# First block's list of work ordered anew, its first two groups of attention cut into three parts

## The chip, the cores and the metric

One core of one Trainium2 chip runs the whole program. The metric is the device time of one execution in microseconds (us); lower is better. In the traces PE is TensorE's matrix multiplication, PEld its weight loads, DVE is VectorE, ACT ScalarE, POOL GpSimd, and SP the engine whose queue issues most DMAs. A "product" below is one matrix multiplication instruction with a moving operand of 512 columns, unless it says idle product (128 columns of fp32).

## The reference, cut to what matters

```python
def _attn_ref(q, k, v):                      # 8 batches, 8 heads, 576 tokens, 64 dims
    scores = scale * np.matmul(q, k.transpose(0, 1, 3, 2))
    # heads 0-3: the last 32 positions; heads 4-7: every 32nd position, both causal
    scores = np.where(masks[None], scores, -1000000000.0)
    scores = scores - np.max(scores, axis=-1, keepdims=True)
    attn = np.exp(scores)
    attn = attn / (np.sum(attn, axis=-1, keepdims=True) + 1e-09)
    return np.matmul(attn, v)

def _moe_ref(x, w_in, w_out):                # 4608 tokens, 512 -> 2048 -> 512
    h = x @ w_in
    g = h * (1.0 / (1.0 + np.exp(-h)))
    return g @ w_out
```

The attention's output, 4608 tokens of 512 features, is the x of the second part. Only the banded or strided keys of a query are computed.

## The kernel before, in words

The 4608 tokens are nine blocks of 512. Every fp32 factor of the large products is split into a high and a low part, so that one true product is three products of rounded parts. Block 0 differs from all later ones: while it runs, the weights are still being loaded, split and kept. Its work is not ordered by a planner inside the program but by a list written out by hand or found by a search, the string `PLAN` (line 143). `Steps.follow` goes through that list word by word and issues each step's instructions; each engine then runs its own instructions in the order of the list, waiting only on what they need. A suffix names the engine of a step that can run on several (`.A` ACT, `.D` DVE, `.P` POOL). After block 0 a planner orders the rest; that order does not depend on the list.

The words of the list. For a group c of attention: `k` loads its queries and keys (SP; the queries of groups 0 to 2 go through ACT's queue), `v` its values, `S` the scores (PE, line 485), `M` adds the mask, finds the row's peak and moves the scores to SBUF (DVE, line 513, two instructions for each of the group's three or four columns of tiles), `E` the exponentials (ACT, line 531, as many), `R` sums and reciprocal (DVE, lines 546 and 547), `N` scales (line 550), `T` transposes (PE, line 556), `P` copies the transposed tile out of PSUM (line 560), `O` multiplies by the values (PE, lines 595 and 600), `Q` scales the local groups' result (DVE, line 639), `X` turns it back (PE, line 662), `B` stores it into x (lines 671 and 655). Groups 0 to 2 are local, 3 to 5 strided; groups 6 to 13 belong to blocks 1 and 2 and have `V`, `F`, `G` in place of `T` and `P`. `C` spreads shared values on POOL (lines 411 to 414). `H` and `L` split x (lines 688 and 692).

For a piece i of the weights: `p` loads it, `a` rounds it on ACT (lines 312 and 317), `j` joins (DVE, line 323), `b` casts the high part (line 368), `d` subtracts for the low part (line 372). For a column fc of the hidden layer: `h` and `i` are its two halves of six products each (line 700), `t`, `g`, `w`, `l` the activation and its split, `o` twelve products into the output (line 759). `z` and `u` store split weights to DRAM for later blocks (SP). `~n` is n idle products with the identity (line 872).

Limits that the list must respect: a load into a key buffer waits for the scores that read it last (group 11 shares its buffer with group 9, so `k11` follows `S9`); a piece's stage waits for the `d` of the piece before it; SP issues in the order of the list. `make_identity` and the masks are made on POOL at the start, in the order: the identity, the plain local mask, its copy for tiles that start a head (used by group 0's first column), another copy, the strided mask.

The last part of `Steps.follow` and of `idle`:

```python
            name, _, engine = word.partition(".")
            step = self[name]
            step.engine = next(e for e in step.costs if e.startswith(engine))
            step.act()
```

Of the kernel before, what the change touches and what calls it, by code (L numbers as in the profile page):

```python
# [25 lines left out]
STRIDE = 32  # L26
# [122 lines left out]
M8 l0.D b2.A S7 i3 a7 k10 a4 p11 j6 d2.D w1.A b6.D j7 j4 t2 b7.A o0 p8 g2 b4.A a9 a11 d7.D d4.D  # L149
l1.D j9 M7 w2.A h4 p13 o1 b9.A l2.D p10 j11 d9.D a8 b11.D t3 i4 p15 E8 g3 d6.D t4 d11.D V6 a10  # L150
S10 w3.D j8 p17 a13 g4 h5 p12 F6.A j10 o2 j13 R8 b10.D b8.A h6 d8.D i5 b13.A l3.D G6.A v6 w4.D
d10.D a15 t5 a17 l4.D i6 p14 u1 M10 a12 j15 p16 u0 j17 d13.D b15.D t6 g6 g5 o3 E7 h7 O6 b17.D
d17.D k9 N8.D a16 w6.A p19 B6 o4 d15.D j12 j16 b12.D h8 l6.D p23 d12.D a14 w5.A b16.D j14 E10 i7
l5.D h9 d16.D V8 t7 p21 R10 a19 k12 b14.D v8 j19 a23 o5 i9 R7 j23 g7 a21 F8.A j21 b23.A i8 G8.A
# [62 lines left out]
def sparse_attention_ffn(ctx: ExitStack, tc: tile.TileContext, kqt, vt, w_in, w_out, out):  # L217
# [214 lines left out]
    class Attention:  # L432


        def __init__(self, b, at):
            self.b, self.at, self.gi = b, at, order_of(b)[at]
            self.by_blocks = b * NG + at >= TURNED
            self.g = g = GROUPS[self.gi]
# [28 lines left out]
        def scores(self, banks=None):  # L467
            g, kbd = self.g, self.kbd
            self.pss = banks or [self.bank("pss") for _ in range(2)]
# [12 lines left out]
            for t, c, rows in self.tiles:  # L482
                for h in range(2):
                    at = slice(h * D, (h + 1) * D)
                    nc.tensor.matmul(  # L485
                        self.pss[h][rows, c * self.seen : (c + 1) * self.seen],
                        kbd[at, 1, g.q0[t] : g.q0[t] + g.rows],
                        kbd[at, 0, g.k0[t] : g.k0[t] + self.seen], start=True, stop=True,
                    )

        def peak(self, part=None):
            g = self.g
            s_ps = self.halves(self.pss)
            if part:
                self.peaks_of(s_ps, (part,))
# [168 lines left out]
        def done(self, engine="ACT"):  # L664
            flat = place_of(self.b).rearrange("p n s -> p (n s)")
            x0 = self.g.first * STRIDE
            dst = flat[:, x0 : x0 + self.cols].rearrange(
                "p (r c q) -> p c r q", c=self.g.n, q=STRIDE
            )
            src = self.psx[:, : self.cols].rearrange("p (c r q) -> p c r q", c=self.g.n, q=STRIDE)  # L670
# [120 lines left out]
    def attention_steps(c, due, last=None):  # L791
# [7 lines left out]
        k = add(f"k{c}", {"SP": P * cols * 4 / RATE}, t0 - 6, [], lambda: load_qk(a),  # L799
                writes=[k_place])  # L800
        s = add(f"S{c}", {"PE": 0.75 if local else 0.68}, t0, [k], a.scores, takes=["ps"] * 2)
        steps.reads(s, k_place)
        m = add(f"M{c}", {"DVE": 0.07 + (0.31 if a.wide else 0.27) * n}, t0 + 1,
                [s, wide_masks] if a.wide else [s], a.peak, takes=["sm", "sum"],
                gives=[s])
        u = m
        if a.spread:
            u = add(f"U{c}", {"POOL": 0.35 + 0.21 * n}, t0 + 1.5, [m], a.lessen)
        cost = 0.1 + 0.11 * n if a.spread else (0.73 if a.wide else 0.667) * n
        e = add(f"E{c}", {"ACT": cost}, t0 + 2, [u], a.weigh)  # L810
# [1636 lines left out]
```

## Time and profile before

| what | value |
|---|---|
| median of 3 runs | 807.0 us (807.0 to 807.51) |
| the profiled execution's own time | 805.44 us |
| its span, first to last instruction | 803.7 us |
| mean granted TensorE clock | 1.000 |
| busy: PE, DVE, ACT, POOL | 99%, 75%, 73%, 14% |
| DMA, mean over the span | 238 GB/s |

Busy shares are means over stages that differ. PE's share counts idle products and matmuls whose ends are modelled. Block 0, the part that the list orders, lies in about the first 130 us. Times in the rows are counted from the first instruction. A timeline row gives the start, the length, the engine, the line, the operation, output and input, the shape and the count, and in brackets the idle time before it and what ended that.

### The profile page before, as it was taken

The numbers are of one execution on the slowest core, as the hardware profiler recorded it, in microseconds if no ns is written. First come the engines' busy times: TensorE is split into PE (matmuls) and PEld (weight loads), VectorE is DVE, ScalarE is ACT, GpSimd is POOL, SyncE is SP. The second block draws the span as 40 slices with busy tenths as digits, with TensorE's granted clock in tenths as the row PEclk, the third lists the DMA queues.
The fourth block names the chain that finished last, engine by engine and source line by source line (L and its number), as shares of the span: only waits on it lengthen the run. The fifth ranks groups of instructions, "written<-read, shape, count | busy, mean of one in ns | idle before, by whom it ended". The sixth has DMA issues, their size and how long they took to land.

```text
span 803.7 us, 18907 instructions
## 1 busy us (share of the span) xinstructions
PE 794.1 (99%) x6661; PEld 658.9 (82%) x6661; DVE 599.2 (75%) x1653; ACT 587.3 (73%) x1574; POOL 112.5 (14%) x160
## 2 busy tenths in 40 slices
PE   8999999999999999999999999999999999999998
PEld 5788778888889898888887888888888888888887
DVE  6999985667878889856779999653799945557653
ACT  7999987557689978898885997788846435545551
POOL 6400004667000000015203000000230000000000
PEclk9999999999999999999999999999999999999999
DMA  8888995566977767899987877986677696666776
GB/s 268 289 271 275 286 287 184 207 235 217 298 244 255 235 225 259 245 323 298 289 263 215 282 249 195 257 266 195 179 192 221 193 272 194 193 196 194 190 218 157
DMA packets 150910, 191.13 MB, mean 238 GB/s; under 512 B 38241, under 2 KB 91105, under 8 KB 150817
## 3 DMA queue, kind: packets, MB, share of 16 engines
q1 hardware_dynamic: 149296, 189.21, 77.1%
q8 instruction: 53, 0.87, 0.4%
q10 hardware_dynamic: 1520, 0.72, 0.3%
q14 instruction: 41, 0.33, 0.1%
HBM read 151.09 MB, written 38.80 MB: 236 GB/s over the span
## 4 chain that ended last, share of the span: by engine, by line
PE 93%; DMA 3%; DVE 1%; ACT 1%; SPq 0%; issue 0%; ACTq 0%
PE ps L1579 34%; PE po L2177 20%; PE po L759 16%; PE ps L700 11%; PE ps L2177 6%; PE ps L615 2%; DMA k<-kqt 1%; PE po L2325 1%; DMA stage<-w_in 1%; PE ps L485 1%; PE ps L476 1%; PE po L615 1%; DMA stage<-w_out 1%; PE po L476 0%; DVE stage L2157 0%; PE po L485 0%
## 5 line engine op out<-in xcount | busy, mean ns | idle before, releaser
L1579 PE MATMUL ps<-xop,w 128*128 128x512 f32 (+1 forms) x720 | 143.7, 348 | 0.0
L1579 PE MATMUL ps<-w,w 128*128 128x512 f32 x576 | 138.6, 390 | 0.0
L1579 PEld LDWEIGHTS ps<-xop,w 128*128 128x128 f32 x720 | 118.1, 189 | 18.5
L1579 PEld LDWEIGHTS ps<-w,w 128*128 128x128 f32 x576 | 107.9, 188 | 22.5
L531 ACT ACTIVATE sm<-sm,sums 128x54 f32<-128x54 f32 (+2 forms) x320 | 109.5, 346 | 5.4 <-DVE sums L513 5.0
L2177 PE MATMUL po<-stage,w 128*128 128x512 f32 x456 | 106.4, 390 | 0.0
L2177 PEld LDWEIGHTS po<-stage,w 128*128 128x128 f32 x456 | 85.4, 188 | 17.8
L700 PE MATMUL ps<-xop,w 128*128 128x512 f32 x384 | 94.0, 392 | 0.0
L700 PEld LDWEIGHTS ps<-xop,w 128*128 128x128 f32 x384 | 71.4, 188 | 15.6 <-DVE th L732 0.4
L531 ACT ACTIVATION_READ_ACCUMULATOR sm<-sm,sums 128x1 f32 x320 | 61.0, 191 | 0.0
L759 PE MATMUL po<-w,ghi 128*128 128x512 f32 x168 | 52.2, 392 | 0.0
L2153 ACT CAST stage<-w 128x512 fp32r<-128x512 f32 x54 | 33.5, 621 | 21.2 <-DVE stage L2157 8.8
L2157 DVE TENSOR_TENSOR stage<-w,stage 128x512 fp32r<-128x512 f32 x54 | 40.0, 745 | 11.2 <-ACT stage L2153 10.6
L2015 DVE TENSOR_TENSOR w<-ps,w 128x512 f32<-128x512 f32 x43 | 29.4, 687 | 24.7 <-PE ps L1579 24.2
L744 DVE TENSOR_TENSOR glo<-th,ghi 128x512 fp32r<-128x512 f32 x48 | 38.4, 803 | 8.6 <-ACT ghi L740 7.0
L582 ACT COPY pt<-sm 32x192 f32<-32x192 f32 (+1 forms) x114 | 41.4, 363 | 4.2 <-DVE sm L574 2.0
L2053 ACT ACTIVATE w<-w 128x512 f32<-128x512 f32 x44 | 27.0, 629 | 17.5 <-DVE w L2015 17.3
L2177 PE MATMUL ps<-stage,w 128*128 128x512 f32 x168 | 39.3, 391 | 0.0
L2177 PEld LDWEIGHTS ps<-stage,w 128*128 128x128 f32 x168 | 31.4, 188 | 6.6
L503 POOL MEMSET sm<- 128x80 f32 (+1 forms) x18 | 2.9, 161 | 239.6 <-ACT pt L582 91.7
L732 DVE SCALAR_TENSOR_TENSOR th<-th,ps 128x512 f32<-128x512 f32 x32 | 21.8, 684 | 19.5 <-ACT th L710 19.4
L2011 ACT COPY w<-ps 128x512 f32<-128x512 f32 x47 | 27.4, 586 | 11.9 <-PE ps L1579 10.7
(327 smaller groups left out, 1629.1 us busy)
## 6 DMA issues: line engine op xcount, KB each, us to landing
w<-sums SPq DMA_DIRECT2D x208, 256.0 KB, 3.3
w<-osums SPq DMA_DIRECT2D x160, 256.0 KB, 3.0
sums<-xop SPq DMA_DIRECT2D x16, 512.0 KB, 3.7
osums<-stage SPq DMA_DIRECT2D x16, 512.0 KB, 5.7
v<-vt SPq DMA_DIRECT2D x21, 384.0 KB, 5.2
stage<-w_out SPq DMA_DIRECT2D x14, 512.0 KB, 4.7
k<-kqt SPq DMA_DIRECT2D x14, 477.0 KB, 5.9
stage<-w_in SPq DMA_DIRECT2D x12, 512.0 KB, 4.9
```

The costliest lines, as they stand in the source:

```text
L531: nc.scalar.activation(out=self.s_sb[:, c, h], in_=self.s_sb[:, c, h], func=AF.Exp, bias=self.peaks[:, c, h : h + 1], scale=-1.0, accum_ou ...
L582: copy[by](out=self.pt[to, odd], in_=of)
L700: nc.tensor.matmul(ph, weight(0, wi, fc)[:, cc // 2, cc % 2 * P : (cc % 2 + 1) * P], x[xi][cc], start=(cc, n) == (0, 0), stop=(cc, n) == ( ...
L744: either[engine].tensor_sub(out=g[1][:, cols], in0=th[:, cols], in1=g[0][:, cols].bitcast(F32))
L759: nc.tensor.matmul(po[tt], g[gi][:, cols], weight(1, wi, fc), start=first and n == 0, stop=last and n == 2,)
L1579: nc.tensor.matmul(bank[:, : right.shape[-1]], left(wi, kt), right[:, kt, xi], start=first and (kt, n) == (0, 0), stop=(kt, n) == (1, 2), ...
L2011: copy_ps(out=unit(place), in_=of())
L2015: nc.vector.tensor_add(out=to, in0=of(), in1=to)
L2053: nc.scalar.activation(out=unit(out), in_=source(), func=AF.Silu)
L2153: copy_ps(out=gated_ops(to.slot)[0], in_=unit(place))
L2157: nc.vector.tensor_sub(out=lo, in0=unit(place), in1=hi.bitcast(F32))
L2177: nc.tensor.matmul(bank(name, key, m), left[:, wi, m * P : (m + 1) * P], right[xi], start=first and (j, i) == (0, 0), stop=(j, i) == (FH - ...
```

## The change

Group 0 gets a class of its own, `Opening`. Its keys and queries lie in DRAM as three parts, one for each of its three columns of four tiles: each part holds 160 columns of keys and 128 of queries, 288 columns of 128 partitions, 144 KB. Before, the keys were one DMA of 208 KB and the queries one of 192 KB. The steps of groups 0 and 1 are cut by column: `S0`, `S51`, `S52` are the scores of group 0's columns, `M0`, `M51`, `M52` and `E0`, `E51`, `E52` theirs in turn; `S1`, `S61`, `S62` and so on are group 1's, which is still loaded as a whole. `k0` and `k52` are issued by SP, `k51` by ACT. The number of scores, of mask and peak instructions and of exponentials stays. Idle products: 25 in place of 24, four in front in place of seven. The rest of the list has the same steps in another order; 27 steps change between ACT and DVE. Code for a spread form that no group used is taken out.

```diff
+class Opening(Group):
+    def __init__(self):
+        super().__init__(True, 0, 12)
+        nk, nq = KW + 3 * STRIDE, 4 * STRIDE
+        self.part = nk + nq
+        self.at = [(t // 4, t % 4) for t in range(self.count)]
+        self.k0 = [self.part * c + STRIDE * r for c, r in self.at]
+        self.q0 = [self.part * c + nk + STRIDE * r for c, r in self.at]
+        self.starts = [(0,), *[()] * (self.n - 1)]
...
+PARTED = (0, 1)
...
 PLAN = """
-k0 k1 k2 v0 ~7 S0 v1 M0 k4 E0 k3 v2 C0 ~1 S1 k5 M1 E1 ~3 S2 M2 p1 E2 v5 T0 P0.D R1 ~7 S4 O0 R0
-M4 E4 Q0 k6 C1 v3 v4 T1 P1.D R2 S3 M3 E3 X0 B0.D a1 T2 P2.D O1 p0 C2 Q1 R4 N4.P S5 M5 k7 O2 X1
-Q2 B1.A R3 N3.D ~2 j1 T4 P4.A E5 H00.D p3 p4 k8 X2 B2.A T3 P3.D a0 L00.P H01.A O4 p5 p2 O3 S6
-b1.D B4 R5 N5.D d1.D j0 b0.A L01.P T5 P5.D d0.D p6 B3 H02.D L02.D ~4 O5 B5 H03.D L03.D a3 M6 j3
-b3.D E6 h0 d3.D Y0 h1 i0 t0 R6 a5 g0 i1 h2 w0.A S8 p7 i2 p9 t1 N6.D j5 b5.D d5.D a2 g1 a6 j2 h3
...
-w7.D d14.D d23.D p22 t9 l7.D p18 z3 z0 a22 t8 o6 N7.D g9 j22 p25 u2 g8 b19.A N10.D S9 V7 O8 a18
-b21.A b22.A F7.A j18 k11 d22.D B8 p20 d19.D p24 z2 z1 M9 d21.D v7 a25 w8.D j25 E9 a20 o7 b25.A
-b18.D h10 d18.D l8.D G7.A S11 V10 a24 i10 d25.D j20 R9 p27 u3 M11 t10 j24 F10.A b24.A h11 g10
...
-g12 p28 z6 R12 N12.D G9.A B10 i13 l11.D w12.A V12 O9 k13 a29 l12.D t13 h14 R11 v11 u7 u6 u5 z7
...
-M13 o12 B11 H10.D H11.D L10.D p30 h15 E13 w14.A H12.A a30 p31 L11.D l13.D R13 l14.D L12.D H13.A
+k0 k51 k52 ~4 S0 M0 S51 M51 S52 ~1 k1 M52 S1 k2 M1 E0 v0 C0 ~2 k4 S61 S62 v1 E51 E52 R0 M61 M62
+T0 E1 E61 S2 E62 ~4 C1 k3 M2 S4 T1 R1 P0.D O0 v2 k5 M4 E2 S3 Q0 P1.D X0 E4 M3 B0.D O1 Q1 S5 T2
+v4 p0 v3 P2.D E3 C2 R2 R4 M5 R3 p1 N4.P E5 ~4 a0 X1 p3 O2 ~3 T4 Q2 N3.D X2 P4.D B1.D v5 R5 H00.D
+~7 T3 j0 O4 B2.A N5.D T5 a1 H01.D P3.A k6 b0.D a3 j1 B4 O3 P5.D d0.D j3 B3 O5 b1.D B5 L00.P
+H02.A p2 H03.A a2 S6 b3.D d1.D L01.P d3.D L02.D p5 p4 a5 h0 L03.D M6 h1 j2 b2.D j5 i0 d2.D Y0 k8
+h2 a4 p7 t0 j4 b5.D E6 g0 b4.A p6 d5.D p9 a6 i1 u0 w0.D p8 l0.D i2 p11 d4.D t1 u1 p10 k7 t2 j6
...
+g7 p20 h9 d22.D p21 B6 g8 a23 V10 G8.A w8.D d19.D S9 w7.A j23 M9 l7.D h10 b23.D i9 a20 N7.D
+F10.A d23.D a21 j21 t9 l8.D G10.A d18.D j20 i10 v8 p24 t10 o7 g9 k11 z6 g10 b21.A a24 p25 O8 E9
+k12 j24 z7 S11 d21.D b24.D o8 w10.D B8 d24.D h11 p26 V7 h12 b20.A R9 a25 l10.D F7.A M11 E11 S12
...
+d28.D o11 v11 g13 G11.A O11 z5 a29 j29 b29.D E13 d29.D w13.D R13 i14 z1 N13.D t14 B11 H10.A
+H11.A g14 h15 l13.D L10.D p30 H12.A a30 H13.A o12 p31 L11.D z2 L12.D j30 i15 w14.D t15 b30.D
+l14.D o13 d30.D L13.D a31 j31 b31.A z0 g15 w15.A d31.D l15.D o14 F12.A V13 G12.A F13.A G13.A
...
+    def load_part(i):
+        some = slice(i * OPENING.part, (i + 1) * OPENING.part)
+        way = nc.scalar.dma_start if i == 1 else load
+        way(out=flat_of(kbds[0])[:, some], in_=flat_of(kqt[0, 0])[:, some])
...
+        if first and a.at in PARTED:
+            es, ss, ms = [], [], []
+            for i in range(n):
+                name = 10 * c + 50 + i if i else c
+                if not i or a.g is OPENING:
+                    size = a.g.part if a.g is OPENING else cols
+                    k = add(f"k{name}", {"SP": P * size * 4 / RATE}, t0 - 6, [],
+                            (lambda i=i: load_part(i)) if a.g is OPENING else lambda: load_qk(a),
+                            writes=[] if i else [k_place])
+                s = add(f"S{name}", {"PE": 0.25}, t0, [k, *ss], lambda i=i: a.scores(only=i),
+                        takes=[] if i else ["ps"] * 2)
+                steps.reads(s, k_place)
+                m = add(f"M{name}", {"DVE": 0.29}, t0 + 1, [s, *ms], lambda i=i: a.peak(only=i),
+                        takes=[] if i else ["sm", "sum"])
+                e = add(f"E{name}", {"ACT": 0.667}, t0 + 2, [m, *es], lambda i=i: a.weigh([i]))
+                ss, ms, es = [*ss[:1], s], [*ms[:1], m], [*es, e]
```

## Rows read from the trace of the kernel before

**Rows 1.** The page's first section: busy time and share of the span.

```profile
PE 794.1 (99%) x6661; PEld 658.9 (82%) x6661; DVE 599.2 (75%) x1653; ACT 587.3 (73%) x1574; POOL 112.5 (14%) x160
```

**Rows 2.** Waits of PE, first 135 us: total, times, longest.

```profile
PE ps L485 <- DMA k<-kqt: 1.0, 1, 1.0
```

**Rows 3.** Chain that ended last, 10 to 150 us: start, length, what.

```profile
41.63 1.36 PE ps L700 x6
42.99 2.72 PE po L759 x12
...
76.90 5.80 DMA k<-kqt
```

**Rows 4.** Busy time of each engine in one stretch of five microseconds.

```profile
20.00:25.00 5.00, 4.53 (x127) 3.37 (x126) 4.64 (x10) 4.80 (x18) 2.19 (x2) 1.00 0.96 305
```

**Rows 5.** Timeline of PE, first 135 us.

```profile
1.35 3.15 PE L872 MATMUL ps<-ident 128*128 128x512 f32 x4 [1.35 <-POOL ident masks.py:199]
4.46 0.72 PE L485 MATMUL ps<-k 64*32 64x64 f32 x48
...
8.53 1.67 PE L872 MATMUL ps<-ident 128*128 128x512 f32 x4
...
22.23 0.72 PE L485 MATMUL ps<-k 64*32 64x64 f32 x48
...
24.81 0.91 PE L600 MATMUL po<-pt,v 64*64 64x54 f32 x24 [0.29 <-ACT xb L655]
25.65 7.11 PE L700 MATMUL ps<-xop,w 128*128 128x512 f32 x30
...
82.83 0.58 PE L485 MATMUL ps<-k 64*64 64x64 f32 x24 [0.98 <-DMA k<-kqt]
...
119.61 0.95 PE L759 MATMUL po<-stage,ghi 128*128 128x512 f32 x2
...
120.63 0.63 PE L759 MATMUL po<-stage,ghi 128*128 128x512 f32 x2
```

**Rows 6.** Timeline of ACT: the first exponential.

```profile
5.60 0.35 ACT L531 ACTIVATE sm<-sm,sums 128x64 f32<-128x64 f32 x1 [2.16 <-DVE sums L513]
```

**Rows 7.** Timeline of DVE, 5 to 25 us.

```profile
5.33 0.22 DVE L513 CUSTOM_DVE_ANT_0 sm<-ps,mask 128x64 f32<-128x64 f32 x1 [5.33 <-PE ps L485]
...
8.24 0.22 DVE L513 CUSTOM_DVE_ANT_0 sm<-ps,mask__94 128x64 f32<-128x64 f32 x1 [0.43 <-PE ps L485]
...
10.13 0.52 DVE L546 TENSOR_SCALAR sums<-sums 128x6 f32<-128x6 f32 x1
...
13.39 0.62 DVE L546 TENSOR_SCALAR sums<-sums 128x6 f32<-128x6 f32 x1
...
15.27 0.55 DVE L671 COPY xb<-po 128x384 f32<-128x384 f32 x1
...
16.73 0.16 DVE L546 TENSOR_SCALAR sums<-sums 128x8 f32<-128x8 f32 x1
...
20.05 0.42 DVE L688 CAST xop<-xb 128x512 fp32r<-128x512 f32 x1
20.38 0.68 DVE L560 COPY pt<-po 128x512 f32<-128x512 f32 x1
20.98 1.12 DVE L368 CAST w<-stage 128x512 fp32r<-128x512 f32 x1
...
22.92 0.69 DVE L372 TENSOR_TENSOR w<-stage,w 128x512 fp32r<-128x512 f32 x1
...
24.17 0.54 DVE L560 COPY pt<-po 128x384 f32<-128x384 f32 x1
```

**Rows 8.** Timeline of POOL: a mask's last instruction, then two longer steps.

```profile
4.12 0.23 POOL L253 TENSOR_SCALAR_AFFINE_SELECT mask<-mask 32x64 f32<-32x64 f32 x1
...
17.31 1.04 POOL L550 TENSOR_TENSOR sm<-sm,sums 128x512 f32<-128x512 f32 x1 [3.33 <-DVE sums L513]
20.55 1.27 POOL L692 TENSOR_TENSOR xop<-xb,xop 128x512 fp32r<-128x512 f32 x1 [2.19 <-DVE xop L688]
```

More of the change, by code (lines that the diff above doesn't have):

```diff
@@ L131 @@
 NG = len(GROUPS)
+class Opening(Group):
[7 more added lines that the diff above has]
+        self.starts = [(0,), *[()] * (self.n - 1)]
+OPENING = Opening()
+PARTED = (0, 1)
 def order_of(b):
@@ L150 @@
[L150 to L154, printed above, removed]
-w7.D d14.D d23.D p22 t9 l7.D p18 z3 z0 a22 t8 o6 N7.D g9 j22 p25 u2 g8 b19.A N10.D S9 V7 O8 a18
@@ new lines @@
+H02.A p2 H03.A a2 S6 b3.D d1.D L01.P d3.D L02.D p5 p4 a5 h0 L03.D M6 h1 j2 b2.D j5 i0 d2.D Y0 k8
+h2 a4 p7 t0 j4 b5.D E6 g0 b4.A p6 d5.D p9 a6 i1 u0 w0.D p8 l0.D i2 p11 d4.D t1 u1 p10 k7 t2 j6
+a9 g1 b6.D d6.D u2 j9 w1.A l1.D R6 a7 a8 h3 p12 o0 S8 j7 i3 o1 b9.A g2 a11 b7.D M8 d7.D t3 j11
+a10 g3 z4 b11.A w3.A w2.A d9.D j8 h4 j10 b10.A b8.A p13 S7 a12 h5 l3.D l2.D N6.D E8 i4 d11.D
+d10.D d8.D p15 i5 M7 j12 V6 o2 b12.D a13 p16 h6 j13 t5 t4 a15 d12.D b13.A g5 u4 g4 j15 a16 u3
+w4.D b15.D k10 d13.D u5 l4.D E7 R8 F6.A p14 o3 i6 d15.D h7 p17 w5.D S10 j16 o4 R7 b16.D p18 p19
@@ new lines @@
+t6 a14 d16.D G6.A p22 N8.D i7 u7 v6 l5.D a17 a18 g6 k9 M10 E10 w6.D j17 j14 j18 b14.A a22 h8
+b17.D a19 l6.D d17.D p23 o5 t7 V8 i8 t8 O6 d14.D j22 F8.A R10 o6 j19 b22.A b18.A N10.D b19.A u6
+g7 p20 h9 d22.D p21 B6 g8 a23 V10 G8.A w8.D d19.D S9 w7.A j23 M9 l7.D h10 b23.D i9 a20 N7.D
+F10.A d23.D a21 j21 t9 l8.D G10.A d18.D j20 i10 v8 p24 t10 o7 g9 k11 z6 g10 b21.A a24 p25 O8 E9
+k12 j24 z7 S11 d21.D b24.D o8 w10.D B8 d24.D h11 p26 V7 h12 b20.A R9 a25 l10.D F7.A M11 E11 S12
+j25 w9.D b25.D i12 N9.D d25.D v10 G7.A l9.D t12 a26 d20.D v7 p27 M12 j26 i11 o9 t11 g11 g12
@@ L382, in vbd_of, with flat_of @@
         return at % (VBUFS if b else VFIRST)
+    def load_part(i):
+        some = slice(i * OPENING.part, (i + 1) * OPENING.part)
+        way = nc.scalar.dma_start if i == 1 else load
+        way(out=flat_of(kbds[0])[:, some], in_=flat_of(kqt[0, 0])[:, some])
+    def flat_of(kbd):
+        return kbd.rearrange("p a t -> p (a t)")
     def load_qk(a):
@@ L437, in __init__ @@
             self.by_blocks = b * NG + at >= TURNED
-            self.g = g = GROUPS[self.gi]
+            self.g = g = GROUPS[self.gi] if b or at else OPENING
             self.spread = b * NG + at in SPREAD
@@ L465, in halves, with scores @@
             return [t[:, : n * keys].rearrange("p (c k) -> p c k", k=keys) for t in banks]
-        def scores(self, banks=None):
+        def scores(self, banks=None, only=None):
             g, kbd = self.g, self.kbd
-            self.pss = banks or [self.bank("pss") for _ in range(2)]
+            ks, qs = (flat_of(kbd),) * 2 if g is OPENING else (kbd[:, 0], kbd[:, 1])
+            if not only:
+                self.pss = banks or [self.bank("pss") for _ in range(2)]
             if self.wide:
@@ L482, in scores @@
             for t, c, rows in self.tiles:
+                if only not in (None, c):
+                    continue
                 for h in range(2):
@@ L486, in scores, with peak @@
                         self.pss[h][rows, c * self.seen : (c + 1) * self.seen],
-                        kbd[at, 1, g.q0[t] : g.q0[t] + g.rows],
-                        kbd[at, 0, g.k0[t] : g.k0[t] + self.seen], start=True, stop=True,
+                        qs[at, g.q0[t] : g.q0[t] + g.rows],
+                        ks[at, g.k0[t] : g.k0[t] + self.seen], start=True, stop=True,
                     )
-        def peak(self, part=None):
+        def peak(self, part=None, only=None):
             g = self.g
             s_ps = self.halves(self.pss)
-            if part:
-                self.peaks_of(s_ps, (part,))
+            if part or only:
+                self.peaks_of(s_ps, (part,) if part else range(2), only)
                 return
@@ L506, in peak, with peaks_of @@
             self.inv = rsum.unsqueeze(3).broadcast_to([P, g.n, 2, self.seen])
-            self.peaks_of(s_ps, range(2) if part is None else (part,))
-        def peaks_of(self, s_ps, hs):
+            self.peaks_of(s_ps, range(2) if part is None else (part,), only)
+        def peaks_of(self, s_ps, hs, only=None):
             for h in hs:
-                for c in range(self.g.n):
+                for c in range(self.g.n) if only is None else (only,):
                     nc.vector.tensor_tensor_reduce(
@@ L666, in done @@
             x0 = self.g.first * STRIDE
[L667 to L670, printed above, removed]
+            dst, src = flat[:, x0 : x0 + self.cols], self.psx[:, : self.cols]
+            if self.g is not OPENING:
+                dst = dst.rearrange("p (r c q) -> p c r q", c=self.g.n, q=STRIDE)
+                src = src.rearrange("p (c r q) -> p c r q", c=self.g.n, q=STRIDE)
             copy[engine](out=dst, in_=src)
@@ L798, in attention_steps @@
         cols = 2 * max(a.g.nq, a.g.nk) if a.b else a.g.nq + a.g.nk
[L799 to L810, printed above, removed]
+        if first and a.at in PARTED:
[14 more added lines that the diff above has]
+                ss, ms, es = [*ss[:1], s], [*ms[:1], m], [*es, e]
+            steps.ends(ss[0], "ps", [m])
+            m = ms[0]
+        else:
+            k = add(f"k{c}", {"SP": P * cols * 4 / RATE}, t0 - 6, [], lambda: load_qk(a),
+                    writes=[k_place])
+            s = add(f"S{c}", {"PE": 0.75 if local else 0.68}, t0, [k], a.scores, takes=["ps"] * 2)
+            steps.reads(s, k_place)
+            m = add(f"M{c}", {"DVE": 0.07 + (0.31 if a.wide else 0.27) * n}, t0 + 1,
+                    [s, wide_masks] if a.wide else [s], a.peak, takes=["sm", "sum"],
+                    gives=[s])
+            e = add(f"E{c}", {"ACT": (0.73 if a.wide else 0.667) * n}, t0 + 2, [m], a.weigh)
+            es = [e]
@@ L811, in attention_steps @@
         if not a.sums_by_pe:
-            cost = 0.39 + 0.13 * n if a.spread else 0.31
-            r = add(f"R{c}", {"DVE": cost}, t1 - 1.5, [e], a.total)
+            r = add(f"R{c}", {"DVE": 0.31}, t1 - 1.5, es, a.total)
         soft = e
@@ L2427 @@
     kq = np.ascontiguousarray(np.stack([columns(k, k_from), columns(q, q_from)], axis=3))
+    local = kq[0, 0].copy()
+    for c in range(OPENING.n):
+        at, nq = c * OPENING.part, 4 * STRIDE
+        nk = OPENING.part - nq
+        kq[0, 0].reshape(P, -1)[:, at : at + nk] = local[:, 0, c * nq : c * nq + nk]
+        kq[0, 0].reshape(P, -1)[:, at + nk : at + nk + nq] = local[:, 1, c * nq : (c + 1) * nq]
     arrays = {
```

8 lines of the change are left out of this document (2 added, 6 removed).

## The prediction

> **What bounds the kernel now.** The page first: PE is busy for 99% of the span, the other engines for 75% or less [rows 1]. So over the whole run only what PE waits for, or what it does without need, can be won. The list under change orders the first 130 us, so I read PE's waits there next: from 25.65 us, when the first product of the hidden layer runs, one wait of size is left, 0.98 us at 82.83 us, for the keys of group 11 [rows 2, 5]. The chain of waits says the same: from 25.65 us it is made of PE's own steps, 1.36 us for six products and 2.72 us for twelve, with one transfer of keys in between [rows 3]. A second, small wait hides in a long row: the first pair of products of `o14` takes 0.95 us where a pair beside it takes 0.63 [rows 5]; the second product of the pair needs the low part of piece 30.
>
> Ahead of 25.65 us PE mostly runs idle products and short steps. There DVE and ACT are the busy ones: 4.64 and 4.80 of 5 us between 20 and 25 us [rows 4]. So the change can win in three places: an earlier `h0`, the wait at 82.83 us, the wait at 119.61 us. What is won there should reach the end, because the order after block 0 does not change and PE stays the bound.
>
> **The cut of group 0.** Now the first scores start at 4.46 us, the first DVE instruction on them at 5.33 us, the first exponential at 5.60 us [rows 5 to 7]. A part of 144 KB stands in place of 208 and 192 KB side by side, so its scores can start earlier, but DVE's first instruction also needs the mask with a head's start, whose last POOL instruction ends at 4.12 + 0.23 = 4.35 us [rows 8]. With the old step of 0.27 us from DVE to ACT the first exponential comes at 4.7 us at best, 0.9 us earlier; at worst, if the three parts share the queues so that none lands sooner, at 5.6 us. I take 4.7 to 5.0 us.
>
> Does `h0` come earlier by that? ACT then has slack, but `h0` also needs what DVE does, and DVE's dense stretch starts with `M2` at 8.24 us, when the scores of group 2 are there [rows 7]. The bytes ahead of group 2's keys are 1294 KB in place of 1278 KB (columns times 512 bytes), so that start stays. From there to the end of `P5`, 24.17 + 0.54 = 24.71 us [rows 7], I count the DVE steps of both lists. Only the old one has `R0` (0.52), `P3` (0.68), `b1` (1.12) and `d1` (0.69): 3.01 us. Only the new one has `P4` (as `P3`, 0.68), `B1` (0.55, the row at 15.27), `H01` and `b0` (each as the cast at 20.05, 0.42): 2.07 us [rows 7]. That is 0.94 us less, since `R0` moves into DVE's wait for group 1's scores.
>
> **Waits of DVE on POOL.** Two old rows are too long for what they do: an add at 13.39 us takes 0.62 us where one at 16.73 takes 0.16, and the cast `b1` at 20.98 takes 1.12 us and ends just after POOL's subtraction of 20.55 to 21.82 us, where the cast at 20.05 takes 0.42 [rows 7, 8]. The first of these (`R2`) comes late enough in the new list to lose its 0.46 us. New candidates: `R1` beside `C0`, 0 to 0.46 us, I take 0.3; `R3` behind `N4`, 0 to 1.04 us: `M5` with six overlapped instructions, about 0.9 us by estimate, lies between, so 0.2; `H01` behind `L00`, 0 to 1.27 us: `j0` and `N5` lie between, together about 1.2 us, so 0.2. `L01` beside `b0` to `d0` has the same bounds; I take 0, as `b0` is queued right behind `H01` and starts first. Here the Trainium skill speaks against the change: its page "SBUF — State Buffer", section "SBUF: two separate sides", has the port pair of VectorE and GpSimd as an exclusive lock for a whole instruction, taken also by a VectorE instruction with two SBUF inputs. The row of `b1` agrees. By that rule `j0` and `N5` too could be held, and the upper bounds, up to 2.5 us for `L00` and `L01`, would count.
>
> So `P5` ends at 24.71 - 0.94 - 0.46 + 0.7 = 24.0 us. Then `O5`, 0.84 us from start to `h0`'s start, and now also `S6`, 0.72 us: it was done at 22.23 us in PE's idle time and now stands between `O5` and `h0` [rows 5]. With 0.1 us from `P5` to `O5`, `h0` starts at 25.66 us: **no gain**. The cut of group 0 buys ACT time that DVE does not pass on.
>
> **Supply after `h0`.** Up to `d5`, which `h3` needs, the new list has on DVE twelve steps of 0.61 us (0.69, overlapped by 0.08 as from 20.38 to 20.98), four casts of 0.4 and `M6`, some 0.9 [rows 7]: 9.8 us from 24.0, so 33.8 us. PE is there after six halves of 1.36 us, at 33.8 us, and needs the low part two products later. No wait, but only some 0.4 us of slack; what DVE loses beyond that PE loses too. Steps that change between ACT and DVE (`w`, `b`) go here at nothing, since ACT has the 0.9 us or more of cover just won; without it each costs one cast.
>
> **The wait at 82.83 us.** `k11` may be issued after `S9`, and took 5.80 us to land [rows 3]. Between `S9` and `S11` PE had one short step, twelve products and six; in the new list it has `h10`, `i9`, `i10`, `o7`, `O8`: 3 x 1.36 + 2.72 + 0.7 = 7.5 us. The transfer is covered with 1.7 us to spare: **-0.98 us**. Bounds: all of it goes, or, if `p24` ahead of `k11` on SP's queue waits long for its stage, it stays or grows by about 1 us.
>
> **The wait at 119.61 us.** `p30` now follows `z5` and `z1` on SP; before it followed `z7` and three `u`. Between `p30` and `o14` PE has more products than before (`o12` moved behind `h15`, 2.72 us). I take the wait as gone, **-0.32 us**; it may stay, or double if `z1` holds the queue. `k10`, `k12` and `p13` also stand behind stores; their scores or products come 2 us or more after the landing that 5.8 us gives, so I put them at nothing; the cover lost, each would be a wait like the one at 82.83 us.
>
> One more or less idle product in PE's idle time costs nothing. **Sum:** 0 - 0.98 - 0.32 = -1.3 us. The profiled execution took 805.44 us, 1.6 us under the median; the sum is a difference within it, and on the median it gives 807.0 - 1.3 = **805.7 us**.
>
> **Rivals.**
> (a) The front comes through: POOL blocks nothing (0.7 us back) and `M2` starts some 0.6 us earlier because group 2 lands earlier. For it: waits in the old front are mostly DVE's and POOL's. Against: the unchanged bytes. `h0` at 24.4 us, sum -2.6: 804.4 us.
> (b) The waits move: one of `k10`, `k12`, `k11` or `p30` lands late. For it: stores in front of loads on SP; against: the products between. About 1 us back: 806.7 us.
> (c) The DVE lock: `L00` and `L01` hold DVE for 1.27 us each, of which 0.2 is in the sum. Then 805.7 + 2.3 = 808.0 us.
> (d) Slower, by TensorE's clock. The seven idle products in front take 3.15 us, seven later ones 1.67 us [rows 5]: the pace of the 1.2 GHz level, then of 2.4, with the rise before the first scores. The new list has four in front, then gaps. If PE stays at the lower level past `S2` and `S4`, scores of 0.72 us, a transpose and four idle products (about 0.95) each take twice as long ahead of `M4`: 0.72 x 3 + 0.5 + 0.95 = 3.6 us, less what lies in gaps: some 3 us on the path to `P5`, so 809 us. It decides if the lower level is still there at 7.5 us. For it: PE has less to do in front than before; against: the scores start earlier. The Trainium skill, "TensorE: Matmul & The Clock Gate", part 1, states such a rise after sustained work and a fall after idling; the two rows agree.
> That the parts do not land earlier is no rival of its own: the sum does not use it.
>
> **How the numbers follow.** Chances: forecast 0.45, (a) 0.25, (b) 0.15, (c) 0.06, (d) 0.09. A measurement of this kernel can tell about 0.2%, 1.6 us, from no change: faster means under 805.4. The forecast's own range is 805.0 to 806.4, some four tenths of it faster. Faster: 0.17 + 0.23 = 0.40. Slower, over 808.6: most of (d), some of (c): 0.11. Same: 0.49. The range reaches from (a) with a little more, 803.9, to past (c), 808.2, and leaves out the most of (d).
>
> **What would show it.** First exponential near 4.7 to 5.0 us; `M2` still near 8.2 us; first product of line 700 near 25.7 us; no wait of PE on keys between 60 and 100 us; no long pair in `o14`. Wrong if line 700 starts before 24.8 or after 26.5 us, if a new wait of PE over 0.5 us shows after it, or if idle products after 5 us still run at 0.45 us each.

## The result and the profile after

| | before | after |
|---|---|---|
| median | 807.25 us (805.65 to 807.65, 6 runs) | 811.17 us (809.15 to 812.42, 6 runs) |
| ratio, 95% interval | | 1.0062 [1.0048, 1.0076] |
| profiled execution, its span | 805.44, 803.7 us | 809.15, 807.4 us |

The kernel became slower; 805.7 us, between 803.9 and 808.2, had been forecast. The two profiled executions lie 3.7 us apart. Everything after block 0 is the same: from the end of `o14` to the end of the span there are 681.0 us in both (803.7 - 122.69 and 807.4 - 126.38). So the 3.7 us arose in block 0, and the question is where.

First the page of the changed kernel (busy time and share) and, under "...", PE's waits between 2 and 60 us (total, times, longest).

```profile
PE 796.1 (99%) x6661; PEld 660.1 (82%) x6661; DVE 599.4 (74%) x1654; ACT 586.9 (73%) x1573; POOL 112.2 (14%) x160
...
PE ps L514 <- issue: 1.7, 1, 1.7
...
PE ps L514 <- DVE sums L542: 1.2, 2, 0.8
PE po L629 <- DVE pt L589: 1.1, 1, 1.1
PE po L585 <- DVE sm L579: 0.9, 1, 0.9
```

The shares are those of [rows 1] within one per cent; they tell nothing of the loss. The waits do, and all lie ahead of the first hidden product, which now starts at 31.08 us, 5.4 us later than in [rows 5]. PE's timeline of the changed kernel (start, length, what, count, and in brackets the idle time before it and its end; L514 scores, L916 idle products, L585 transposes, L629 strided values, L729 hidden layer, L788 output layer):

```profile
3.40 0.47 PE L514 MATMUL ps<-k 64*32 64x64 f32 x16
4.67 0.61 PE L514 MATMUL ps<-k 64*32 64x64 f32 x16 [0.80 <-DVE sums L542]
5.64 0.60 PE L514 MATMUL ps<-k 64*32 64x64 f32 x16 [0.36 <-DVE sums L542]
6.18 0.79 PE L916 MATMUL ps<-ident 128*128 128x128 f32 x2
7.11 0.47 PE L514 MATMUL ps<-k 64*32 64x64 f32 x16
7.50 1.22 PE L916 MATMUL ps<-ident 128*128 128x256 f32 x2
8.65 0.68 PE L514 MATMUL ps<-k 64*32 64x64 f32 x32
9.27 0.90 PE L585 MATMUL po<-ident,sm 128*128 128x128 f32 x3
10.10 0.85 PE L514 MATMUL ps<-k 64*32 64x64 f32 x48
...
12.55 0.55 PE L585 MATMUL po<-ident,sm 128*128 128x128 f32 x3
...
18.40 0.27 PE L514 MATMUL ps<-k 64*64 64x64 f32 x1 [1.67 <-issue]
...
26.86 0.52 PE L585 MATMUL po<-ident,sm 128*128 128x128 f32 x3 [0.95 <-DVE sm L579]
...
29.59 0.91 PE L629 MATMUL po<-pt,v 64*64 64x54 f32 x24 [1.14 <-DVE pt L589]
30.43 0.73 PE L514 MATMUL ps<-k 64*32 64x64 f32 x48
31.08 0.50 PE L729 MATMUL ps<-xop,w 128*128 128x512 f32 x1
...
123.66 0.61 PE L788 MATMUL po<-stage,ghi 128*128 128x512 f32 x2
```

The same stretch of the kernel before, from group 1's first scores to group 2's (`S2`, 7.47 us):

```profile
5.54 0.30 PE L485 MATMUL ps<-k 64*32 64x64 f32 x2
...
7.47 0.75 PE L485 MATMUL ps<-k 64*32 64x64 f32 x48
```

Group 0's first column starts 1.06 us earlier than the whole group did, but the second and third wait for DVE's peaks of the column ahead, and group 1's scores come at 7.11 us in place of 5.54. Three transposes take 0.90 us at 9.27 and 0.55 us at 12.55: PE stands at its 1.2 GHz level far longer than in [rows 5] (the granted clock in the trace rises at 10.61 us; before, at 4.18 us). Line 729 has a first product at 31.08, and `o14` an ordinary first pair of 0.61 us, where [rows 5] show 0.95.

DVE's timeline of the changed kernel (L542 peaks, L579 scale, L385 and L340 cast and join of weights, L589 copy out of PSUM):

```profile
4.39 0.23 DVE L542 CUSTOM_DVE_ANT_0 sm<-ps,mask 128x64 f32<-128x64 f32 x1 [4.39 <-POOL mask L270]
...
11.00 0.23 DVE L542 CUSTOM_DVE_ANT_0 sm<-ps,mask__94 128x64 f32<-128x64 f32 x1 [0.88 <-PE ps L514]
...
19.18 0.56 DVE L589 COPY pt<-po 128x384 f32<-128x384 f32 x1 [1.89 <-PE po L585]
...
20.24 0.17 DVE L542 CUSTOM_DVE_ANT_0 sm<-ps,mask_strided 128x64 f32<-128x64 f32 x1
...
25.08 1.63 DVE L579 TENSOR_TENSOR sm<-sm,sums 128x384 f32<-128x384 f32 x1
...
26.97 0.41 DVE L385 CAST w<-stage 128x512 fp32r<-128x512 f32 x1
27.31 1.76 DVE L340 SCALAR_TENSOR_TENSOR stage<-stage 128x512 int32<-128x512 int32 x1
28.99 0.55 DVE L589 COPY pt<-po 128x384 f32<-128x384 f32 x1
```

And POOL's, the subtractions `L00` and `L01`:

```profile
24.64 1.66 POOL L721 TENSOR_TENSOR xop<-xb,xop 128x512 fp32r<-128x512 f32 x1 [3.10 <-DVE xop L717]
27.13 1.38 POOL L721 TENSOR_TENSOR xop<-xb,xop 128x512 fp32r<-128x512 f32 x1 [0.83 <-DVE xop L717]
```

Read the two together. `N5` (25.08) and `j1` (27.31) run in POOL's two subtractions and end 0.4 and 0.6 us behind them. They take 1.63 and 1.76 us; `N5` took 0.56 us in the kernel before and another join of the new list, at 24.48 us, takes 0.68. `P5`, behind both, holds up the last products of `O5`.

**The loss in three stretches**, by these rows and [rows 7]: up to `M2`, 11.00 in place of 8.24 us, **2.76 us**; from `M2` to `M5`, 9.24 us in place of 8.81 (`M5` was at 17.05 us), **0.43 us**; from `M5` to the first hidden product, 10.84 us in place of 8.60, **2.24 us**. Together 5.43 us. Behind it some 1.7 us come back.

### The profile page after: what moved, and what is told of

Its sections match the earlier page's. It is cut to its first block, busy times and chain, and to the rows that moved or that the text cites. A ratio compares the mean times of both kernels' runs of the same rounds, so it can differ in the third digit from the quotient of the medians.

```text
span 807.4 us, 18924 instructions
## 1 busy us (share of the span) xinstructions
PE 796.1 (99%) x6661; PEld 660.1 (82%) x6661; DVE 599.4 (74%) x1654; ACT 586.9 (73%) x1573; POOL 112.2 (14%) x160
## 4 chain that ended last, share of the span: by engine, by line
PE 96%; DVE 2%; issue 1%; POOL 0%; ACT 0%; POOLq 0%
PE ps L1623 34%; PE po L2221 20%; PE po L788 17%; PE ps L729 11%; PE ps L2221 6%; PE ps L644 2%; PE ps L514 2%; PE po L2369 1%; PE ps L503 1%; PE po L644 1%; DVE sm L542 1%; PE po L503 0%; DVE stage L2201 0%; PE po L514 0%; ACT stage L2197 0%
## 5 line engine op out<-in xcount | busy, mean ns | idle before, releaser
L729 PE MATMUL ps<-xop,w 128*128 128x512 f32 x384 | 93.2, 392 | 0.0
L729 PEld LDWEIGHTS ps<-xop,w 128*128 128x128 f32 x384 | 71.5, 188 | 15.3
L788 PE MATMUL po<-w,ghi 128*128 128x512 f32 x168 | 52.3, 392 | 0.0
L739 ACT ACTIVATE th<-ps 128x512 f32<-128x512 f32 x32 | 18.9, 595 | 24.2 <-PE ps L729 23.6
```

The source lines that it names most:

```text
L729: nc.tensor.matmul(ph, weight(0, wi, fc)[:, cc // 2, cc % 2 * P : (cc % 2 + 1) * P], x[xi][cc], start=(cc, n) == (0, 0), stop=(cc, n) == ( ...
L788: nc.tensor.matmul(po[tt], g[gi][:, cols], weight(1, wi, fc), start=first and n == 0, stop=last and n == 2,)
```

## The experiments

The runs of the kernel before that stood beside them had medians of 805.66 (first four kernels), 806.19 (next four) and 805.9 us (last three). Ratios are against these. "First product" is the first of the hidden layer. Words of the lists are shown as diffs.

**1. Seven idle products in front** of the changed kernel.

```diff
-k0 k51 k52 ~4 S0
+k0 k51 k52 ~7 S0
```

> The changed kernel with seven idle products in front of the first scores in place of four; nothing else differs. Clock theory: the rise to the upper level comes near 4.2 us as before the change (10.6 us in the changed kernel's profile), M2 starts 1 to 2 us earlier than its 11.0 us, the first hidden product at 29 to 30.2 us in place of 31.1, and the time is 1 to 2 us lower, near 809 to 810 us, with less spread between runs. Rival, that the scores waiting for the peaks of the column before alone set the front: the first scores start 1.1 us later, everything after as late or later, no gain or 1 us slower.

1.0057 [1.0042, 1.0072], 810.2 us. The clock still rose at 10.71 us, the first product came at 31.88. Seven idle products only pushed `S0` to 4.65 us; in this list, with the scores in single columns behind them, they did not bring the early rise back in this execution. The gain of the clock theory did not come; the rival's no gain did.

**2. The scores of all columns ahead of the peaks.**

```diff
-S0 M0 S51 M51 S52 ~1 k1 M52 S1 k2 M1 E0 v0 C0 ~2 k4 S61 S62 v1 E51 E52 R0 M61 M62
+S0 S51 S52 M0 M51 k1 M52 ~1 S1 S61 S62 k2 M1 E0 v0 C0 ~2 k4 v1 E51 E52 R0 M61 M62
```

> The changed kernel with the scores of a group's three columns issued together and the peaks behind them, so that no score waits for a peak of its own group. Theory of the scores that wait: the two waits of PE on DVE before 6 us (0.80 and 0.36 us) and DVE's five waits on PE (4.1 us together) shrink; M2 starts near 9 us in place of 11.0, the time falls by 1 to 2 us. Clock theory alone: PE's steps stay as slow as they are, M2 moves by less than 0.7 us, the time by less than 0.7 us.

1.0043 [1.0027, 1.0059], 808.57 us. In PE's timeline of this kernel the waits for DVE give way to waits for keys:

```profile
5.39 0.47 PE L513 MATMUL ps<-k 64*32 64x64 f32 x16 [1.34 <-DMA k<-kqt]
...
7.89 0.96 PE L513 MATMUL ps<-k 64*32 64x64 f32 x48 [1.31 <-DMA k<-kqt]
```

The third part was there at 5.39 us only, later than the whole group in the kernel before (`S0` at 4.46), and group 1's keys at 7.89 us. `M2` stayed late, at 11.56 us, and the first product at 31.61; the interval of the time overlaps the changed kernel's (1.0048 to 1.0076), and no gain is shown. So the waits for the peaks hid a later supply. The changed kernel's own transfers agree: the same 224 KB of group 1's load, issued second on SP's queue before and third now, took longer to land. The issues of the first 2.2 us (queue, count, KB, us to landing) of the kernel before:

```profile
k<-kqt SPq DMA_DIRECT2D x1, 224.0 KB, 3.8
```

and of the changed one:

```profile
k<-kqt SPq DMA_DIRECT2D x1, 224.0 KB, 5.3
```

The thirteen traces of this document agree on it: where that load is second on SP's queue (the kernel before and runs 4, 5 and 7 to 11) it took 3.7 to 4.2 us, where it is third (the changed kernel and runs 1, 2, 3 and 6) 5.3 to 6.2.

**3. `L00` and `L01` on DVE**, behind `d0`, in the changed kernel.

```diff
-d0.D j3
+d0.D L00.D L01.D j3
...
-L00.P
...
-L01.P
```

> The changed kernel with L00 and L01, the low parts of x, on DVE right behind d0 in place of POOL. Lock theory: N5 and j1 take 0.55 and 0.69 us in place of 1.63 and 1.76, which is 2.1 us less for DVE, against 1.2 us for the two subtractions that it now makes itself; P5 ends 2.1 us earlier, the first hidden product comes at 29 to 29.7 us in place of 31.1 and the time falls by 0.7 to 1.5 us. Rival, that those two long rows are covered by other waits: the first hidden product stays or comes later and the time stays or rises by up to 1.2 us.

1.0039 [1.0023, 1.0055], 808.55 us. DVE's timeline of this kernel:

```profile
25.34 0.62 DVE L578 TENSOR_TENSOR sm<-sm,sums 128x384 f32<-128x384 f32 x1
...
26.70 0.75 DVE L339 SCALAR_TENSOR_TENSOR stage<-stage 128x512 int32<-128x512 int32 x1
```

`N5` and `j1` are back at 0.62 and 0.75 us. `N5` starts 0.26 us later than in the changed kernel, yet `P5` ends at 27.91 in place of 29.54 us and the first product comes at 29.46 in place of 31.08. The two subtractions on POOL cost 1.6 us there, near what the lock theory gave them; the interval of the time still touches the changed kernel's.

**4. The kernel before with four idle products in front.**

```diff
-k0 k1 k2 v0 ~7 S0
+k0 k1 k2 v0 ~4 S0
```

> The kernel before with four idle products in front in place of seven and nothing else. Clock theory: PE idles from 3.2 us to the landing of group 0, the rise comes later than 4.2 us, PE's first scores and transposes take up to twice as long, and the time rises by 0.5 to 2.5 us with a wider spread. Rival, that in the old list PE has slack enough in front: under 0.4 us either way.

1.0006 [0.9993, 1.0019], 805.51 us: no difference that can be told. The clock rose at 7.67 us, 3.5 us later, and the first product came at 26.00, 0.35 us later. In this order the late rise is cheap by itself.

This run says more of the forecast's gains. Four windows, each from the first hidden product to the end of `o14` (window, length, PE's busy time, the other engines' and, behind the clock, DMA): the kernel before,

```profile
25.65:122.69 97.04, 96.00 (x847) 76.47 (x845) 90.60 (x283) 90.19 (x253) 5.63 (x13) 1.00 0.88 281
```

the changed kernel,

```profile
31.08:126.38 95.30, 95.30 (x852) 76.60 (x845) 91.11 (x285) 89.38 (x254) 3.67 (x9) 1.00 0.87 269
```

the old list with four idle products,

```profile
26.00:121.58 95.58, 95.58 (x848) 76.45 (x845) 90.53 (x283) 90.02 (x253) 5.61 (x13) 1.00 0.90 284
```

and the old list with its group 0 cut (6, below):

```profile
28.28:123.54 95.26, 95.26 (x848) 76.53 (x845) 90.73 (x283) 89.92 (x253) 5.42 (x13) 1.00 0.89 280
```

PE is busy throughout in the last three. The old order has no wait on group 11's keys either: in run 4 that load, in the window from 74 to 86 us, landed sooner than the 5.80 us of [rows 3]:

```profile
k<-kqt SPq DMA_DIRECT2D x1, 359.0 KB, 4.3
```

So the waits of 0.98 and 0.32 us in [rows 2, 5] do not stand in every execution of the old order. Each comes once more among its five traces (the kernel before and runs 4, 6, 7 and 11): the wait on group 11's keys in run 7, the long first pair of `o14` in run 11.

```profile
85.11 0.58 PE L513 MATMUL ps<-k 64*64 64x64 f32 x24 [0.87 <-DMA k<-kqt]
```

```profile
119.85 0.95 PE L758 MATMUL po<-stage,ghi 128*128 128x512 f32 x2
```

None of the seven traces of the new order (the changed kernel and runs 1, 2, 3, 8, 9 and 10) has either.

**5. The old front with the new rest**: the first 163 words of the old list, then the new list's order, groups whole. No diff is short here: up to `j9` the old list stands; what is left follows in the order of the new one.

> The kernel before with its own list up to about o0 and h4 (163 words), followed by the new list's order for all that is left; group 0 and group 1 are not cut. Theory that the front alone loses and the rest of the new list gains: the first hidden product stays near 25.7 us, the waits of PE at 82.8 us (0.98) and at o14 (0.32) are gone, the time is 0.7 to 1.5 us under the kernel before. Rival, that the rest of the new list gained only because PE came 5 us late to it: the waits come back elsewhere, within 0.5 us of the kernel before or slower.

1.002 [1.0012, 1.0029], 807.68 us: slower. The first product came at 26.05 us, but the window from there to the end of `o14` took 98.88 us:

```profile
26.05:124.93 98.88, 97.80 (x847) 76.18 (x845) 91.66 (x284) 91.57 (x258) 5.62 (x13) 1.00 0.86 268
```

PE's waits there are three of 0.3 us, and PE's busy time is 2.2 us over that of run 4; which products are longer was not followed up. The new rest gains nothing behind an early first product. The join is a list of its own, so this speaks less surely of the new rest than the windows above.

**6. The cut alone**: the old list, with the parts' words put beside those of their groups.

```diff
-k0 k1 k2 v0 ~7 S0 v1 M0 k4 E0 k3 v2 C0 ~1 S1 k5 M1 E1
+k0 k51 k52 k1 k2 v0 ~7 S0 S51 S52 v1 M0 M51 M52 k4 E0 E51 E52 k3 v2 C0
+~1 S1 S61 S62 k5 M1 M61 M62 E1 E61 E62
```

> The changed kernel's cut of groups 0 and 1 (load in three parts, scores, peaks and exponentials by column) in the old order of the list, with the old seven idle products in front. Transfer theory: the second part on SP's queue pushes group 1's keys to about 7 us (5.35 before, 7.0 in the changed kernel), group 1's peaks start 0.7 to 1.5 us later, and the first hidden product comes 0.5 to 1.5 us late; the time rises by 0.5 to 1.5 us. Rival, that the order of the list alone lost the front: the first hidden product within 0.4 us of 25.7, the time within 0.4 us of the kernel before.

1.0016 [1.0001, 1.0031], 807.12 us. `M1` at 9.15, `M2` at 11.41 us (6.85 and 8.24 before), the first product at 28.28. The cut by itself makes the groups behind it late, in the old order too. Group 1's 224 KB, third on SP's queue here, took 6.2 us from an issue at 1.66 us, and PE waited ahead of its scores until they were there (the row names another load that landed by then):

```profile
8.03 0.96 PE L513 MATMUL ps<-k 64*32 64x64 f32 x48 [2.42 <-DMA v<-vt]
```

Here the granted clock also rose, fell at 7.66 us in the gap ahead of group 1 and rose again at 11.07, so the loss of 2.6 us holds both.

**7. As 6, with two of the three parts on ACT's queue.**

```diff
-        way = nc.scalar.dma_start if i == 1 else load
+        way = nc.scalar.dma_start if i else load
```

> The run before this one (the cut in the old order) with the third part of group 0 on ACT's queue in place of SP's, so that each queue holds one DMA less ahead of group 1's keys. Transfer theory: group 1's keys land before 6.2 us again, its peaks start at least 0.7 us earlier than with the part on SP, and the time is 0.3 to 1.2 us lower than there. Rival, that the bytes and not the queue decide: group 1 lands within 0.4 us of the run with the part on SP.

1.0006 [0.9995, 1.0018], 806.65 us; `M1` at 8.38, `M2` at 10.05. Of the 3.2 us that 6 had lost at `M2`, 1.4 came back, with an earlier rise of the clock (6.34 us) among it. Group 1's keys took 4.0 us again, but its queries, now third on ACT's queue, took 5.7 in place of 3.5 us, and its scores still waited:

```profile
7.51 0.71 PE L513 MATMUL ps<-k 64*32 64x64 f32 x48 [0.97 <-DMA k<-kqt]
```

The wait had moved to the other queue. The first product, at 28.38 us, did not follow: ahead of the last products of `O5` PE stood 1.32 us with nothing in the profile to release it ("issue"). `M5` came at 18.43 us, 1.4 later than in the kernel before, with no fall of the clock in this trace. By its time run 7 is not told apart from run 6 or from the kernel before.

**8. The new list mended**: as 7 in its queues, scores ahead of peaks as in 2, seven idle products as in 1, `S2` ahead of `T0`, `L00` and `L01` as in 3.

> The changed kernel with all suspected costs of its front mended at once: third part of group 0 on ACT's queue, scores of a group's columns together, seven idle products in front and three more before the scores of group 2, which stand ahead of T0, and L00 and L01 on DVE behind d0. If these are the causes of the 5.4 us by which the first hidden product came late: it comes at 26 to 28 us in place of 31.1 and the time is within 1.3 us of the kernel before. If something else holds the front: later than 28.5 us, and slower than the kernel before by over 1.3 us.

1.003 [1.0015, 1.0046], 808.34 us. In the profiled execution the first product came at 26.81 us, 4.3 us earlier than in the changed kernel, and the end of `o14` at 122.79, as before. The first product came as forecast, the time did not (2.2 us over the kernel before, where at most 1.3 was forecast). The profiled execution took 806.88 us, with a wait of PE of 1.0 us behind block 0 ("issue") that neither the kernel before nor the changed one has; two of the other executions took 810.2 and 811.5 us, and what they lost was not recorded. So the causes mended here account for the late first product, and a part of the loss over all runs stays open.

**9. The order alone**: the new list without the words of the parts, groups whole.

```diff
-k0 k51 k52 ~4 S0 M0 S51 M51 S52 ~1 k1 M52 S1 k2 M1 E0
+k0 ~4 S0 M0 ~1 k1 S1 k2 M1 E0
```

> The order of the new list alone: the groups stay whole, as in the kernel before, and the words of the parts 51, 52, 61 and 62 are taken out of the new list; all of the reference is computed. Theory (the cut and the order each cost a part of the 5.4 us at the first product of the hidden layer, and the parts add): the cut alone put that product at 28.3 us where it had been at 25.65, so the order alone should cost the other 2.8 us: first product at 28.0 to 29.0 us, the add N5 or the cast after it (line of j) again held by over 0.8 us behind a subtraction of POOL, end of o14's products near 124, time 807.5 to 809. Rival (the order costs only because the parts come late, so that without the cut it is as good as the old one): first product at 25.5 to 26.5 us, 805.5 to 806.5.

1.003 [1.0016, 1.0044], 808.03 us. The first product came at 30.02 us, later than forecast. The parts do not add there: 2.6 us by the cut (run 6) and 4.4 by the order are more than the 5.4 of both. DVE's timeline shows the same two held instructions, without any cut:

```profile
24.02 1.64 DVE L549 TENSOR_TENSOR sm<-sm,sums 128x384 f32<-128x384 f32 x1
...
26.25 1.76 DVE L322 SCALAR_TENSOR_TENSOR stage<-stage 128x512 int32<-128x512 int32 x1
```

PE's timeline shows a fall of the clock in front: behind a wait of 0.84 us the granted clock fell to its lower level at 16.43 us, until 19.84, and four idle products (the second row) took 1.92 us. The changed kernel's longer wait of 1.67 us had no such fall behind it, so that the gap made the clock fall is not shown.

```profile
16.22 0.27 PE L484 MATMUL ps<-k 64*64 64x64 f32 x1 [0.84 <-issue]
...
17.11 1.92 PE L871 MATMUL ps<-ident 128*128 128x512 f32 x2
```

**10. As 9, with seven idle products and `L00`, `L01` on DVE.**

> As the run before it (new order, groups whole), with seven idle products in front in place of four and the low parts L00 and L01 on VectorE, behind d0, in place of GpSimd. Theory (VectorE's waits for GpSimd were 1.6 us of the order's cost): first product of the hidden layer 1 to 2 us earlier than in the run before it, at 26.5 to 27.5 us, and 806 to 807.5. If the lists differ in nothing but that lock: 25.5 to 26 us and 805 to 806. Rival (the order itself is late, by S6 ahead of the product and by what VectorE does before P5): as late as the run before it, within 0.5 us.

1.0011 [0.9998, 1.0025], 806.34 us: 1.7 us less than 9. DVE's timeline:

```profile
24.28 0.62 DVE L549 TENSOR_TENSOR sm<-sm,sums 128x384 f32<-128x384 f32 x1
...
25.57 0.68 DVE L322 SCALAR_TENSOR_TENSOR stage<-stage 128x512 int32<-128x512 int32 x1
```

The clock rose at 4.24 us, `M2` came at 8.86 (9.73 in run 9), the first product at 28.26 us, again later than forecast, behind a wait of PE of 1.76 us ("issue") ahead of `S5`'s last scores. The new order with its lock mended is at best as good as the old one.

**11. The old list with `L00`, `L01` on DVE**, four idle products.

```diff
-N5.D d1.D j0
+N5.D d1.D L00.D j0
...
-P5.D d0.D p6
+P5.D d0.D L01.D p6
```

> The kernel before with four idle products in front in place of seven, and the low parts L00 and L01 on VectorE, the one behind d1, the other behind d0, in place of GpSimd. The cast b1 took 1.12 us beside GpSimd's subtraction where one takes 0.42 without. Theory (the lock costs the old list too, 0.7 us at b1): b1 takes 0.45 us or less, the two subtractions cost 0.3 to 0.7 us each on VectorE instead, of which only the first lies ahead of P5: first product of the hidden layer 0 to 0.4 us earlier, time within 0.1 per cent of the kernel before. Rival (the subtractions hold up VectorE as much as the lock did, or more): first product 0.3 to 0.8 us later, time 0.05 to 0.15 per cent longer.

1.0003 [0.9994, 1.0013], 806.32 us. DVE's timeline, `b1` and the first subtraction:

```profile
21.87 0.51 DVE L367 CAST w<-stage 128x512 fp32r<-128x512 f32 x1
...
24.05 0.75 DVE L691 TENSOR_TENSOR xop<-xb,xop 128x512 fp32r<-128x512 f32 x1
```

`b1` went from 1.12 to 0.51 us, and the subtraction put 0.75 on DVE ahead of `P5`; the first product came at 26.88, 0.88 us later than in run 4. In time a draw. No version beat the kernel before.

## Why the prediction was wrong, point by point

**"The bytes ahead of group 2's keys ... so that start stays" failed first.** `M2` came 2.76 us late. The sum counted bytes, not the order in which queues take them and who waits. (The bytes too were miscounted: by the sizes of the loads in the traces, group 2's own among them, they are 3 x 144 + 224 + 208 + 2 x 192 = 1248 KB in place of 208 + 224 + 208 + 3 x 192 = 1216, 32 KB more and not 16.) By the rows of the two timelines, 1.57 us of it arose ahead of group 1's scores (7.11 in place of 5.54 us), 1.06 from there to group 2's scores (2.99 us in place of 1.93, with the rest of group 1's scores and `T0` in between and a part of it at the lower clock), and 0.13 behind them. Group 1's scores were held twice over: by the columns, which wait for each other's peaks, 0.80 and 0.36 us, and by its keys, which landed about as PE was free for them, 5.3 us after their issue in place of 3.8. That the landing alone is enough is shown by run 2, where without the first wait the second takes its place, and by run 6; that the place on the queue sets it, by the thirteen traces. That the cut costs time is shown by run 6 (1.0001 is its lower bound, so just) and by run 9 beside the changed kernel (1.0030 against 1.0062, intervals apart). What was forecast of the cut itself held: the mask's 4.35 us bounded it, `M0` ran at 4.39 and the first exponential started in ACT's timeline, against [rows 6], at

```profile
4.65 0.35 ACT L560 ACTIVATE sm<-sm,sums 128x64 f32<-128x64 f32 x1 [1.22 <-DVE sums L542]
```

It helped nobody, as the forecast said.

**"Waits of DVE on POOL" was the right mechanism, mis-sized.** The forecast gave `L00` 0.2 us, because `j0` and `N5` would lie between it and `H01`, and `L01` nothing, because `b0` would start first. Both came true, and the lock took the step in between and the step behind: `N5` lost 1.07 us (1.63 - 0.56) and `j1` about 1.07 (1.76 - 0.69, with the 0.69 of such a step in [rows 7]). Together 2.14 us. This is rival (c), which had a chance of 0.06. The 2.24 us lost from `M5` on are a net: 1.64 up to the end of `P5` (9.30 us in place of 7.66), where fewer steps of DVE make up for a part of the lock, and 0.60 behind it, where `S6` stands. Run 3, with the subtractions on DVE behind `d0`, took 1.6 us back. The casts, which the forecast feared for (`H01`, `b0`), ran in 0.41 us. That `R1` beside `C0` would lose 0.3 us was right: its first instruction took 0.46 at 11.87 us, where one takes 0.16. `R3` behind `N4` lost 0.35 (0.51 at 21.06 us) where 0.2 was given. By the Trainium skill, "SBUF — State Buffer", section "SBUF: two separate sides", of a VectorE instruction with two SBUF inputs and a GpSimd instruction that reads SBUF, whichever starts first has the shared port pair for its whole length and the other waits. Both held steps have two such inputs and end 0.4 and 0.6 us behind POOL's subtractions: the trace agrees. The forecast had quoted that rule and then taken the value between the ends that its own count of steps preferred.

**Rival (d), the clock, was real; its price over all runs stays open.** The lower level stayed past 7.5 us, its deciding point. It was priced at 3 us. In the profiled executions the old list with a rise 3.5 us later lost 0.35 us at the first product (run 4), and the new one 0.87 us at `M2`, with three idle products of difference besides (8.86 in run 10, 9.73 in run 9). Over all executions it may be dearer. Of the changed kernel's six, the two at a mean granted clock of 0.999 took 809.15 and 809.75 us, the four at 0.997 and 0.996 took 810.9 to 812.4; in run 3 the two at 0.996 took 810.5 and 811.7, the three at 1.000 took 807.3 to 808.6. Run 1 does not show it (809.9 at 1.000, 810.2 and 810.45 at 0.996 and 0.995), nor does run 7. That a longer stretch at the lower level makes the slower executions of the changed kernel is argued from that, not shown.

**From `M2` to `M5`** the forecast's terms come to -0.68 us (`R0` -0.52, `R2` -0.46, `R1` +0.3); 0.43 us were lost. PE stood 1.67 us ahead of the last score of `S5`, with no releaser that the profile shows, and DVE 1.89 us behind it. The trace has a fetch of 16 KB of instructions on queue q8 from 15.47 to 16.99 us, which ends as this wait begins; the kernel before has two shorter waits of this kind there, 0.57 and 0.49 us. The wait varies from execution to execution: with the new order from under 0.25 us (run 2) to 1.76 (run 10), with the old from 0.33 (run 11) to 1.21 (run 7). In run 2 `M5` came 8.39 us after `M2`, yet the first product no sooner, with a fall of the clock at 29.41 us ahead of it. No run took the fetch away, so its cause is argued, and what the wait cost the first product is open.

**`S6` ahead of the first product** was counted right: 0.72 us by the forecast, 0.65 measured (30.43 to 31.08).

**"-0.98" and "-0.32" were gains on waits that the old order has in some executions only.** In the changed kernel both are gone as forecast, no new wait stands behind the first product, and its window is 1.74 us shorter than that of the kernel before. But the old order is as short where it is without them (95.26 and 95.58 us, against 95.30). Of its five traces two have the first and two the second. They were read from a single trace and put at their full length on the median. Had all else held, only a part of the 1.3 us could have been won there; how large a part is not shown.

**The sum.** 5.43 us lost in front, 1.74 shorter behind: 3.7 us between the profiled executions. Over all runs, the order alone costs 0.30%, the cut alone 0.16%, both 0.62%; the intervals leave open whether the two do more together.

## What to carry to other kernels

A wait on a transfer that stands in one trace need not stand in the next: look at several executions of the same order, or at the spread of that transfer's landings, before putting its whole length into a sum. When a load is cut and put ahead of others, follow what is queued behind it on the same queue to its landing and count the waits there; nearly equal bytes are no reason. When a GpSimd instruction with SBUF operands is placed beside a dense stretch of VectorE, price it at its full length on whichever two-input step stands next, and try it on VectorE first.

## What was not expected of the hardware

The granted clock's first rise lay anywhere between 4.18 and 13.56 us in the thirteen traces, though PE's work began at 1.35 us in the kernel before and at 1.36 in the changed one. With seven idle products in front it came at 4.18, 4.24, 4.25, 4.59, 5.71, 6.34 and, in run 1, at 10.71 us; with four at 7.67, 9.05, 9.60, 10.61, 12.34 and 13.56 us. So the three idle products that the change took out, and that the forecast's sum put at nothing, go with a later rise in all but one trace; run 4 shows that by itself this costs the old order nothing that can be told. The clock could also fall again in front (runs 2, 6, 9 and 10), while the mean over the span still read 0.997 or more.

A POOL subtraction that meets a DVE step grows too: `L00` took 1.66 us in the changed kernel, where it started while a join ran on DVE, and 1.27 in [rows 8].
